# Fused attention and SwiGLU kernel: a third exp buffer, a lagged and re-timed prologue, and the second batch's attention placed earlier

## The chip, the cores and the metric

The kernel runs on one core of one Trainium2 chip. The metric is the device time of one execution in microseconds (us). Engines are named as the profile names them: PE is the matmul engine (PEld its weight loads), DVE is VectorE, ACT is ScalarE, POOL is GpSimd, SP is SyncE. In these traces PE, DVE, ACT and POOL each work through their own instructions in the order in which they were issued (in the hole shown below, a copy on DVE whose input was ready at 87.04 us began at 90.28 us, behind two scalings and a product).

## The reference

Attention over 8 batches, 12 heads, 448 positions and head size 64, with one extra term in the denominator, feeds a feed-forward network (FFN) on 3584 rows of 768:

```python
scores = scale * np.matmul(q, k.transpose(0, 1, 3, 2))
m = np.max(scores, axis=-1, keepdims=True)
e = np.exp(scores - m)
attn = e / (np.sum(e, axis=-1, keepdims=True) + np.exp(-m) + 1e-09)
o = np.matmul(attn, v)                                     # (8, 12, 448, 64)
x = o.transpose(0, 2, 1, 3).reshape(B * S, H * D)          # (3584, 768)
rms = np.sqrt(np.mean(x * x, axis=-1, keepdims=True) + 1e-06)
xn = x / rms * rms_g
g = xn @ w_gate                                            # 768 x 1536
silu = g * (1.0 / (1.0 + np.exp(-g)))
out = silu * (xn @ w_val) @ w_out                          # 1536 x 768
```

All inputs and the output are fp32. The kernel works in bf16 on PE.

## The kernel before

The program has a prologue and a main part. In the prologue the attention of batch 0 is computed alone, with dummy ("warm") matmuls at its start. The main part is the FFN, written as a list of steps: a gate or value step (`TA`, six matmuls of 448 columns, and a tanh on ScalarE for the gate) and an output step (`TB`, twelve matmuls of 384). A counter `now` adds up the steps' nominal lengths, and a timetable `ops` says at which value of `now` each piece of the other batches' attention is put between two FFN steps. I call the units of `now` FFN units, counted from the first FFN matmul. One is close to a microsecond of FFN work; the attention put between the steps comes on top (in the changed kernel the scaling set at 16.5 begins at 83.21 us, 43.8 us after the first FFN matmul).

The work of a head pair: transpose q and k on PE (`emit_T`) and copy the result out of PSUM (the memory that holds PE's results) on VectorE (`pair_t`); four chunks of scores on PE, each followed by one exp on ScalarE into `p_sb`; then the two heads' weighted sums on PE against v, which carries a column of ones for the denominator (`emit_AV`), and a reciprocal and a multiply on VectorE, which fill `x_sb`. After six pairs: sums of squares, a root, the scaling of x by row, transposes on PE, and then the FFN of that batch can start.

```python
    p_bufs = []
    v_bufs = []
    for i in range(2):
        p_i = consts.tile([128, C * 2 * S + PAD], BF16, name=f"p_sb{i}")
        nc.vector.memset(p_i[96:128, 0:2 * S + PAD], 1.0)
        nc.vector.memset(p_i[:, C * 2 * S:], 0.0)
        p_bufs.append(p_i)
        v_i = consts.tile([128, C, H, E1], BF16, name=f"v_sb{i}")
        # ... memsets of v_i ...
    # ... cut ...
        def exps():                                   # inside scores(g, c)
            p_v = p_bufs[g % 2][0:P, c * 2 * S:(c + 1) * 2 * S].rearrange("p (h q) -> p h q", h=2)
            nc.scalar.activation(out=p_v, in_=s_ps[0:P, :, 0:S], func=AF.Exp, scale=scale)
        return exps

    def emit_S(g, half):
        catch_up()
        pend = [scores(g, c) for c in (2 * half, 2 * half + 1)]
        pend[0]()
        put_off.append(pend[1])
        if not late[0]:
            catch_up()
    # ... cut ...
    def emit_scale(b, c):
        nc.vector.tensor_scalar(out=xn_tiles[b][:, c, :], in0=x_tiles[b][:, c, :],
                                scalar1=xnt_tiles[b, "r"][:, c:c + 1], scalar2=None,
                                op0=ALU.mult)
    # ... cut: the timetable; emit_T(6..13) and pairs 6..11 are batch 1 ...
    spans = {2: (24, 58), 3: (58, 90), 4: (90, 136), 5: (136, 172), 6: (172, 214), 7: (214, 251)}
    for j, t0 in enumerate((0.0, 1.2, 3.5, 5.8, 13.6, 15.9, 21.5, 25.0)):
        ops.append((t0, lambda j=j: emit_T(NP + j)))
    for j, t0 in enumerate((1.1, 3.4, 5.7, 8.0, 14.8, 17.1)):
        ops += [(t0 + 0.56 * i, op) for i, op in enumerate(micro_ops(NP + j))]
    ops.append((20.6, lambda: emit_stats(1, 1)))
    ops.append((20.7, lambda: emit_root(1)))
    ops.append((23.0, lambda: (emit_scale(1, 0), emit_scale(1, 1))))
    ops.append((24.1, lambda: (emit_scale(1, 2), emit_scale(1, 3))))
    for c in range(C):
        ops.append((25.2 + 0.01 * c if c < 2 else 26.3 + 0.01 * c, lambda c=c: emit_turn_x(1, c)))
    for i in range(2 * KD):
        ops.append((5.0 + 0.7 * i, lambda: scale_w(1)))
    # ... cut: casts on GpSimd, among them v, q and k of batch 2 at 22.5 to 22.7 ...
    now = 0.0
    for t, f in ffn:
        late[0] = t == TA
        while ops and ops[0][0] <= now:
            ops.pop(0)[1]()
        f()
        catch_up()
        # ... steps of later batches ...
        now += t
```

With `late` set, a step of two score chunks issues only its first exp; the second is held until after the next FFN step, so on ScalarE it stands behind that step's tanh.

The softmax here doesn't subtract the row's maximum and nothing guards it: scores larger than these inputs give would overflow.

## Time and profile before

| | before |
|---|---|
| median of the first 3 runs | 489.59 us (488.14 to 489.92) |
| span of the profiled run | 486.9 us, mean granted PE clock 0.986 |
| first FFN matmul | 41.91 us |
| PE idle in the hole at 81 to 95 us | 3.88 us, clock 0.88 |

The first part of the profile page gives busy time, share of the span and instruction count of each engine:

```profile
PE 462.1 (95%) x4041; PEld 248.1 (51%) x4041; DVE 247.3 (51%) x620; ACT 245.7 (50%) x357; POOL 101.4 (21%) x123
```

PE is the bound, with all others near half. So the question is where its last 5% goes. The windows view cuts the span into stretches of one's choosing. Its columns are: stretch, length, busy time of each engine (with instruction counts), granted PE clock (1.00 is full), DMA share, GB/s. For the prologue, the FFN of batch 0, the start of batch 1's FFN, and the last batches:

```profile
core 0: us, PE busy (x) PEld busy (x) DVE busy (x) ACT busy (x) POOL busy (x), PEclk, DMA share, GB/s
0.00:41.91 41.91, 32.40 (x401) 18.50 (x402) 27.75 (x79) 23.88 (x31) 25.75 (x41) 0.88 1.11 195
41.91:81.00 39.09, 38.83 (x439) 20.50 (x439) 27.20 (x67) 25.67 (x34) 7.55 (x10) 1.00 0.59 114
81.00:95.20 14.20, 10.32 (x92) 5.24 (x90) 11.28 (x22) 5.31 (x11) 12.19 (x15) 0.88 0.69 135
...
356.89:454.32 97.43, 96.26 (x709) 51.95 (x708) 45.73 (x110) 38.08 (x60) 2.68 (x4) 1.00 0.19 44
```

Length minus PE busy is PE's idle time: 9.51, 0.26, 3.88 and 1.17 us. The prologue and the hole stand out. The timeline shows the gap in each. Its columns are: start, duration, engine, line, operation, output and inputs with shapes, count, and in brackets the idle time before it with what ended that. First the prologue:

```profile
12.56 0.58 PE L174 MATMUL qkt_ps<-identity,k_bf 112*64 112x112 bf16 x8 [1.12 <-DMA k_bf<-in_k_dram]
...
13.68 0.92 ACT L206 ACTIVATE p_sb_117<-s_ps 112x896 bf16<-112x896 f32 x1 [2.38 <-PE s_ps L201]
...
27.78 3.34 ACT L206 ACTIVATE p_sb_117<-s_ps 112x896 bf16<-112x896 f32 x4
```

PE stands at the transposes of a head group whose k has not landed, and ScalarE has no scores for 2.38 us. The last exp of batch 0 ends at 27.78 + 3.34 = 31.12 us. Then the hole:

```profile
86.37 3.47 DVE L261 TENSOR_SCALAR xn<-x_sb,rinv 112x768 bf16<-112x768 bf16 x2
...
87.59 1.05 POOL L150 CAST q_bf<-q_f 112x1024 bf16<-112x1024 f32 x1
88.57 1.05 POOL L150 CAST k_bf<-k_f 112x1024 bf16<-112x1024 f32 x1
...
90.95 0.72 PE L270 MATMUL xnt_ps<-identity,xn 112*128 112x112 bf16 x6 [3.51 <-DVE pair_t_107 L177]
91.46 2.44 PE L302 MATMUL v_ps<-xnt_sb,wv_bf 128*128 128x448 bf16 x6
```

Two scalings of x take 3.47 us while GpSimd casts; the pair copy and the transposes queue behind them, PE waits 3.51 us, and its next six FFN matmuls take 2.44 us, about twice the 1.29 to 1.31 us of such a group elsewhere. The waits view of 300 to 490 us (engine, line, what it waited for, us in total, times, longest) has one longer wait and seven short ones of the kind of its second line here:

```profile
PE g_ps L302 <- DMA xnt_sb<-xn: 1.2, 1, 1.2
PE g_ps L302 <- DVE silu_5892 L308: 0.2, 1, 0.2
...
```

### The profile page before, as it was taken

What the parts mean: (1) busy time and instruction counts of PE and PEld (TensorE: products, weight loads), DVE (VectorE), ACT (ScalarE), POOL (GpSimd) and SP (SyncE); (2) the same over time, 40 slices, a digit from 0 to 9 for tenths busy, and PEclk for the clock granted to TensorE, in tenths of its full rate; (3) what the DMA queues carried; (4) which work ended last, traced back from release to release, by engine and by line L of the source; (5) the groups of instructions that cost most, each with busy time, mean ns of one, the idle gap of its engine ahead of it and who ended that gap; (6) DMA issues with size and microseconds to landing.
All of it is one profiled execution on the core that took longest, in us unless ns stands there. A gap on an engine that the chain in (4) does not pass through costs nothing.

```text
span 486.9 us, 9856 instructions
## 1 busy us (share of the span) xinstructions
PE 462.1 (95%) x4041; PEld 248.1 (51%) x4041; DVE 247.3 (51%) x620; ACT 245.7 (50%) x357; POOL 101.4 (21%) x123
## 2 busy tenths in 40 slices
PE   6988999799999999999999999999999999999995
PEld 2544555345455554544555554444555554455563
DVE  4586778645635166755633155745643156555200
ACT  4764755456556565545555655455556552122221
POOL 7454401801403031322003121313010001000000
PEclk9789999899999999999999999999999999999999
DMA  8999750999929997386039988189014320300133
GB/s 144 215 221 200 146 113 1 171 217 201 213 62 225 178 276 152 44 191 126 1 71 232 222 216 151 24 184 184 8 34 104 86 66 7 51 1 0 34 97 98
DMA packets 86905, 60.48 MB, mean 124 GB/s; under 512 B 50774, under 2 KB 81820, under 8 KB 86860
## 3 DMA queue, kind: packets, MB, share of 16 engines
q1 hardware_dynamic: 73820, 43.60, 42.2%
q0 software_dynamic: 13040, 16.26, 18.6%
q8 instruction: 31, 0.51, 0.5%
q14 instruction: 14, 0.11, 0.1%
HBM read 47.19 MB, written 11.01 MB: 120 GB/s over the span
## 4 chain that ended last, share of the span: by engine, by line
PE 81%; DVE 10%; ACT 3%; DMA 2%; issue 1%; POOL 1%; DVEq 0%; ACTq 0%; POOLq 0%
PE o_ps L327 23%; PE g_ps L302 19%; PE v_ps L302 18%; PE u_ps L231 9%; PE s_ps L201 8%; DVE xsq L254 3%; PE s_ps L302 3%; ACT t_sb L306 2%; DVE xn L261 1%; DMA k_bf<-in_k_dram 1%; DVE ht_sb L313 1%; DVE x_sb L235 1%; PE qkt_ps L174 1%; DMA xnt_sb<-xn 1%; ACT p_sb_117 L206 0%
## 5 line engine op out<-in xcount | busy, mean ns | idle before, releaser
L302 PE MATMUL v_ps<-xnt_sb,wv_bf 128*128 128x448 bf16 x576 | 126.0, 355 | 2.5 <-DVE ht_sb L313 2.4
L327 PE MATMUL o_ps<-wo_bf,ht_sb 128*128 128x384 bf16 x672 | 116.5, 326 | 0.4 <-DVE silu_2063 L308 0.4
L302 PE MATMUL g_ps<-xnt_sb,wg_bf 128*128 128x448 bf16 x504 | 109.3, 353 | 3.7 <-DMA xnt_sb<-xn 1.2
L206 ACT ACTIVATE p_sb_111<-s_ps 112x896 bf16<-112x896 f32 x96 | 84.0, 915 | 21.3 <-PE s_ps L201 21.2
L306 ACT ACTIVATE t_sb<-g_ps 128x448 f32<-128x448 f32 x84 | 45.6, 543 | 95.1 <-PE g_ps L302 94.8
L206 ACT ACTIVATE p_sb_117<-s_ps 112x896 bf16<-112x896 f32 x96 | 83.8, 915 | 16.8 <-PE s_ps L201 16.6
L327 PEld LDWEIGHTS <-ht_sb 128*128 128x128 bf16 x672 | 62.8, 98 | 46.8 <-issue 8.3
L302 PEld LDWEIGHTS <-wg_bf 128*128 128x128 bf16 x576 | 52.2, 97 | 58.4 <-issue 15.6
L302 PEld LDWEIGHTS <-wv_bf 128*128 128x128 bf16 x576 | 52.8, 98 | 54.8 <-issue 12.1
L330 ACT ACTIVATE out_sb<-o_ps 128x384 f32<-128x384 f32 x56 | 27.5, 490 | 66.4 <-PE o_ps L327 61.5
L234 DVE RECIPROCAL recip<-u_ps 112x4 f32<-112x4 f32 x96 | 17.0, 178 | 84.3 <-PE u_ps L231 84.3
L285 POOL TENSOR_TENSOR rinv<-ms,neghalf 112x2 f32<-112x2 f32 x16 | 10.9, 706 | 160.1 <-DVE ms L281 160.1
L235 DVE TENSOR_TENSOR x_sb<-u_ps,recip 112x256 bf16<-112x256 f32 x96 | 40.8, 424 | 3.3
L150 POOL CAST q_bf<-q_f 112x1024 bf16<-112x1024 f32 x17 | 17.7, 1041 | 100.0 <-DMA q_f<-in_q_dram 86.6
L201 PE MATMUL s_ps<-qk_t 64*128 64x448 bf16 x272 | 37.5, 354 | 0.0
L254 DVE CUSTOM_DVE_ANT_0 xsq<-x_sb 112x512 bf16<-112x512 bf16 (+1 forms) x60 | 36.7, 612 | 1.6
L231 PEld LDWEIGHTS <-p_sb_117 112*128 112x128 bf16 (+1 forms) x768 | 30.1, 99 | 11.7 <-issue 3.9
L231 PEld LDWEIGHTS <-p_sb_111 112*128 112x128 bf16 (+1 forms) x768 | 30.0, 99 | 9.8 <-issue 3.8
L150 POOL CAST k_bf<-k_f 112x1024 bf16<-112x1024 f32 x17 | 17.9, 1054 | 13.2 <-DMA k_f<-in_k_dram 13.2
L261 DVE TENSOR_SCALAR xn<-x_sb,rinv 112x768 bf16<-112x768 bf16 x32 | 19.8, 649 | 0.1
L201 PEld LDWEIGHTS <-qk_t 64*128 64x128 bf16 x272 | 7.8, 94 | 21.2 <-issue 20.4
L231 PE MATMUL u_ps<-v_sb_114,p_sb_117 112*128 112x65 bf16 (+1 forms) x384 | 16.9, 197 | 1.6 <-DVE x_sb L235 1.3
(265 smaller groups left out, 347.7 us busy)
## 6 DMA issues: line engine op xcount, KB each, us to landing
q_f<-in_q_dram SPq DMA_DIRECT2D x15, 448.0 KB, 4.8
k_f<-in_k_dram SPq DMA_DIRECT2D x15, 448.0 KB, 6.1
v_f<-in_v_dram SPq DMA_DIRECT2D x15, 448.0 KB, 7.0
v_f<-in_v_dram POOLq DMA_DIRECT2D x9, 448.0 KB, 7.8
out_dram<-out_sb SPq DMA_DIRECT2D x8, 336.0 KB, 3.4
wg_bf<-in_moe_w_gate_dram POOLq DMA_DIRECT2D x6, 384.0 KB, 11.5
wv_bf<-in_moe_w_val_dram POOLq DMA_DIRECT2D x6, 384.0 KB, 13.7
wo_bf<-in_moe_w_out_dram POOLq DMA_DIRECT2D x3, 768.0 KB, 18.1
```

The lines of the kernel that those rows point to most:

```text
L150: eng.tensor_copy(out=dst, in_=staged[n, i].rearrange("p h c d -> p c h d"))
L201: nc.tensor.matmul(s_ps[:, hh, 0:S], lhsT=k_t[r, k0:k0 + 128], rhs=qs[r], start=True, stop=True)
L206: nc.scalar.activation(out=p_v, in_=s_ps[0:P, :, 0:S], func=AF.Exp, scale=scale)
L231: nc.tensor.matmul(u_ps[:, qc, :], lhsT=p_sb[0:K, q0:q0 + 128], rhs=v_sb[0:K, c, h, :], start=(c == 0), stop=(c == C - 1))
L234: nc.vector.reciprocal(out=recip, in_=u_ps[0:P, :, D:E1])
L235: nc.vector.tensor_tensor(out=x_tiles[b][:, :, h * D:(h + 1) * D], in0=u_ps[0:P, :, 0:D], in1=recip.to_broadcast([P, C, D]), op=ALU.mult)
L254: nc.vector.tensor_tensor_reduce(out=xsq[:, 0:cols.stop - cols.start], in0=x_c, in1=x_c, scale=1.0, scalar=0.0, op0=ALU.mult, op1=ALU.add, ...
L261: nc.vector.tensor_scalar(out=xn_tiles[b][:, c, :], in0=x_tiles[b][:, c, :], scalar1=xnt_tiles[b, "r"][:, c:c + 1], scalar2=None, op0=ALU. ...
L302: nc.tensor.matmul(ps[:, 0:S], lhsT=w[:, dk, m * 128:(m + 1) * 128], rhs=xnt_tiles[b][:, :, dk, :], start=(dk == 0), stop=(dk == KD - 1))
L306: nc.scalar.activation(out=t, in_=ps[:, 0:S], func=AF.Tanh, scale=0.5)
L327: nc.tensor.matmul(o_ps[:, 0:HN], lhsT=ht_tiles[b2][:, fk, c * 128:(c + 1) * 128], rhs=wo_bf[:, fk, n * HN:(n + 1) * HN], start=(fk == 0), ...
L330: nc.scalar.activation(out=o_sb[:, n * HN:(n + 1) * HN], in_=o_ps[:, 0:HN], func=AF.Copy, scale=0.5)
```

## The change

Its intent: get batch 0 to its FFN sooner, by giving q and k of the next head groups the first place among the loads, letting the weighted sums run two pairs behind the scores (which needs a third exp buffer), and filling PE with dummy matmuls where it would idle; close the hole, by finishing batch 1 earlier, so that its scaling comes before GpSimd's casts; and let gate results go to the score banks as soon as the last scores are done. x is scaled in place, which saves a buffer. Cut to its core:

```diff
+    NPB = 3
-    for i in range(2):
+    for i in range(NPB):
         p_i = consts.tile([128, C * 2 * S + PAD], BF16, name=f"p_sb{i}")
         nc.vector.memset(p_i[96:128, 0:2 * S + PAD], 1.0)
 # ... v buffers: still two; weights loaded three 128-row blocks at a time instead of two ...
-    def scale_w(n):
+    def scale_w(n, eng):            # ScalarE or VectorE
 # ...
-            p_v = p_bufs[g % 2][0:P, ...]
+            p_v = p_bufs[g % NPB][0:P, ...]
 # ... sums of squares of batch 0 in three parts: heads 0-5, 6-9, 10-11 ...
-        nc.vector.tensor_scalar(out=xn_tiles[b][:, c, :], in0=x_tiles[b][:, c, :],
+        nc.vector.tensor_scalar(out=x_tiles[b][:, c, :], in0=x_tiles[b][:, c, :],
 # ...
-        if b == B - 1 and part == 0:
+        if scores_done[0] and part == 0:
             ps = ps_s.tile([128, 2, 512], FP32, name="s_ps")[:, 0, :]
 # ... the timetable ...
-    for j, t0 in enumerate((0.0, 1.2, 3.5, 5.8, 13.6, 15.9, 21.5, 25.0)):
+    for j, t0 in enumerate((2.3, 3.4, 5.6, 7.2, 8.8, 10.4, 18.6, 22.0)):
         ops.append((t0, lambda j=j: emit_T(NP + j)))
-    for j, t0 in enumerate((1.1, 3.4, 5.7, 8.0, 14.8, 17.1)):
-        ops += [(t0 + 0.56 * i, op) for i, op in enumerate(micro_ops(NP + j))]
-    ops.append((20.6, lambda: emit_stats(1, 1)))
-    ops.append((20.7, lambda: emit_root(1)))
-    ops.append((23.0, lambda: (emit_scale(1, 0), emit_scale(1, 1))))
-    ops.append((24.1, lambda: (emit_scale(1, 2), emit_scale(1, 3))))
+    for j, t0 in enumerate((4.0, 5.6, 7.2, 8.8, 10.4, 12.0)):
+        ops += [(t0 + 0.39 * i, op) for i, op in enumerate(micro_ops(NP + j))]
+    ops.append((14.9, lambda: (emit_stats(1, 1), emit_root(1))))
     for c in range(C):
-        ops.append((25.2 + 0.01 * c if c < 2 else 26.3 + 0.01 * c, lambda c=c: emit_turn_x(1, c)))
+        ops.append((16.5 + 0.6 * c, lambda c=c: emit_scale(1, c)))
+        ops.append((18.7 + 1.1 * c, lambda c=c: emit_turn_x(1, c)))
     for i in range(2 * KD):
-        ops.append((5.0 + 0.7 * i, lambda: scale_w(1)))
+        ops.append((9.0 + 0.45 * i, lambda: scale_w(1, V)))
-    # ... GpSimd: casts of batch 2 at 22.5 to 22.7 and 29.0
+    # ... GpSimd: casts of batch 2 at 19.5 and 19.6 and 26.0; load_w(4), the second
+    #     weight half, at 3.7 (before: in the prologue)
 # ... the prologue ...
+    between = {
+        (0, 0): [lambda: emit_T(1), lambda: [load_qkv(2, i, G) for i in range(2)]],
+        (0, 1): [gains, lambda: warm(1)], (0, 2): [lambda: warm(2)], (0, 3): [lambda: warm(2)],
+        (1, 0): [lambda: warm(2)], (1, 1): [lambda: warm(2)],
+        (1, 2): [lambda: emit_T(2), lambda: cast_qkv(0, 2, V)],
+        # ...
+        (2, 1): [lambda: emit_AV(0, 0)], (2, 2): [lambda: emit_AV(0, 1)],
+        # ... and so on, two pairs behind the scores ...
+    }
     for g in range(NP):
-        for op in micro_ops(g):
-            op()
+        for c in range(C):
+            scores(g, c)()
+            for f in between[g, c]:
+                f()
```

The transposes of batch 1's first pair (0.0 before, 2.3 after) move from just before the first FFN matmul to behind it.

## The prediction

> **What bounds the kernel now.** The matmul engine (PE). By the windows view it is busy 32.4 of the first 41.9 us (before the first FFN matmul), 38.8 of the next 39.1, 10.3 of 14.2 between 81.0 and 95.2 us, and 380.6 of the last 391.8 (some 5 us of that idle is the tail). Apart from dummy warm-up matmuls, PE work is the same after the change. So three things can move the time: the start of the first FFN matmul (41.9 us), the hole at 81 to 95 us, and small PE waits elsewhere.
>
> **Prologue.** ScalarE runs 24 exps, 0.81 us each back to back, from 7.1 us. In the timeline they end at 31.1 us, though 24 x 0.81 = 19.5: some 4 us are lost, 2.4 where PE stood at the third pair's transposes until q and k of the second head group landed (12.5 us), the rest mostly because PE then ran at half clock (mean 0.66 from 10 to 20 us; 16 weighted-sum matmuls took 1.0 us against 0.6 later). The Trainium skill (TensorE: Matmul & The Clock Gate, "What's actually happening") says idle PE is re-throttled; the trace agrees. The change loads v later, transposes later, adds warm-up matmuls and lags the weighted sums, so exps lose that gap. The price: a third exp buffer puts one more 0.8 us VectorE memset ahead of the first transposed copy (+1 us); VectorE is nearly full from 20 to 31 us (0.55 us per head's scaling, copies 0.54, casts 0.60, squares 0.46 to 0.72), and the last pair's copy queues among squares, so the last exps slip 1 to 2 us. The chain after the last weighted sum (sums, root, scaling 4 x 0.73 us, transposes) stays about 8 us. First FFN matmul: 39.0 us (37.5 to 40.5), gain 2.9.
>
> **Hole.** VectorE's scaling of x took 1.7 us a piece there against 0.73 in the prologue, while GpSimd ran casts; PE waited 3.5 us and its clock fell (six matmuls 2.24 us instead of 1.14). Whole loss about 5.3 us. The Trainium skill (GPSIMD Engine Reference, "1. Specifications") says GpSimd shares its SBUF interfaces with VectorE; 1.7 against 0.73 us fits. The change finishes batch 1 some 6 FFN units earlier and puts scaling ahead of the casts: gain 5 us.
>
> **Given back.** Batch 1's attention is pressed from 19 into 10 FFN units. There PE needs about 22 us and ScalarE 21 (24 exps, 4 tanh of 0.45): I expect 2 us (0.5 to 4) of new PE waits for exps. The second weight half lands near 60 us, needed at 59 to 66: no wait, little slack.
>
> **Elsewhere.** Gate results move to the score banks one batch earlier: seven waits of 0.2 us go; one of 1.2 us for transposed x should go: about -2 us. Scaling in place adds no wait.
>
> **Sum.** 489.6 - 2.9 - 5 + 2 - 2 = 481.7 us; range 477.5 to 486. Faster by over 2% 0.27, within 2% 0.71, slower 0.02.
>
> **What would show it.** Right: no 2.4 us gap between exps; first FFN matmul near 39 us; waits for exps of 1 to 3 us in the first 25 us of the FFN; no PE wait over 1 us up to 110 us; no waits on silu in the last two batches. Wrong: first FFN matmul after 41 us, or PE waiting for weight scaling.
>
> **What would make it wrong.** First-half weights landing after 31 us; the dense stretch costing 4 us or more; VectorE less full in the prologue than I think (then 478); another hole at batch 1's transposes.

## The result, and the profile after

Ratios here and below are the mean time of one kernel's runs over the mean of the other's runs of the same rounds, so not quite the ratio of the medians.

| | before | after |
|---|---|---|
| median (runs) | 489.75 us (488.14 to 489.92, 4) | 485.76 us (485.36 to 486.50, 4) |
| ratio, 95% interval | | 0.9927 [0.9903, 0.9952] |
| span of the profiled run | 486.9 us, clock 0.986 | 483.3 us, clock 0.994 |
| first FFN matmul | 41.91 us | 39.41 us |

The change gains about 3.6 us by the ratio (0.0073 x 489), where 7.9 were forecast. Busy times by engine after:

```profile
PE 460.6 (95%) x4053; PEld 247.9 (51%) x4056; DVE 242.0 (50%) x625; ACT 250.6 (52%) x363; POOL 98.4 (20%) x119
```

That page line hardly moves, so the averages are no help. The windows view of the same stages does show it (columns as before):

```profile
0.00:39.41 39.41, 31.43 (x397) 16.90 (x401) 25.94 (x81) 27.30 (x35) 18.60 (x32) 1.00 1.00 178
39.41:79.06 39.65, 34.20 (x415) 18.58 (x415) 23.69 (x61) 25.59 (x34) 11.38 (x15) 0.96 0.74 142
79.06:95.20 16.14, 14.63 (x126) 7.50 (x123) 12.25 (x29) 7.54 (x14) 11.12 (x13) 1.00 0.48 113
...
356.97:451.21 94.24, 94.24 (x706) 51.98 (x705) 45.31 (x108) 38.12 (x60) 2.68 (x4) 1.00 0.18 45
```

PE's idle time is now 5.45 us in the FFN of batch 0 (0.26 before), 1.51 in the former hole (3.88 before), and none in the last batches (1.17 before). The waits view of 39 to 110 us names the new idle time:

```profile
PE s_ps L205 <- ACT p_sb_108 L210: 2.2, 3, 1.1
PE s_ps L205 <- ACT p_sb_111 L210: 1.4, 3, 0.6
PE u_ps L235 <- DVE x_sb L239: 1.3, 1, 1.3
PE s_ps L205 <- DVE pair_t_102 L181: 1.1, 1, 1.1
```

With one more of 0.21 us, seven waits for exps sum to 3.8 us. The timeline at their worst place shows the queue on ScalarE:

```profile
46.27 0.92 ACT L210 ACTIVATE p_sb_108<-s_ps 112x896 bf16<-112x896 f32 x1 [2.03 <-PE s_ps L205]
46.35 1.31 PE L310 MATMUL g_ps<-xnt_sb,wg_bf 128*128 128x448 bf16 x6
...
47.69 0.54 ACT L314 ACTIVATE t_sb<-g_ps 128x448 f32<-128x448 f32 x1 [0.51 <-PE g_ps L310]
48.13 2.52 ACT L210 ACTIVATE p_sb_108<-s_ps 112x896 bf16<-112x896 f32 x3
...
49.10 0.37 PE L205 MATMUL s_ps<-pair_t_102 64*128 64x448 bf16 x2 [1.14 <-ACT p_sb_108 L210]
...
50.71 0.55 PE L205 MATMUL s_ps<-pair_t_104 64*128 64x448 bf16 x2 [0.44 <-ACT p_sb_108 L210]
51.19 2.42 PE L310 MATMUL v_ps<-xnt_sb,wv_bf 128*128 128x448 bf16 x6
```

ScalarE waits 2.03 us for the first scores of the pair, does one exp, idles another 0.51 us for the gate, and only then meets three exps in a row, for which PE has to wait: there are two score banks, and both are full. It was idle 2.5 us just before it became the bottleneck. The six matmuls at 51.19 took 2.42 us, so PE's clock had also been halved.

The hole is nearly gone. One wait is left there, for the copy of a transposed pair (the last line of this cut of the timeline; the lines before it show scalings of x and a cast):

```profile
83.21 0.42 DVE L266 TENSOR_SCALAR x_sb<-x_sb,rinv 112x768 bf16<-112x768 bf16 x1 [0.20 <-POOL rinv L293]
...
83.80 1.03 POOL L154 CAST v_sb_117<-v_f 112x1024 bf16<-112x1024 f32 x1
84.07 2.08 DVE L266 TENSOR_SCALAR x_sb<-x_sb,rinv 112x768 bf16<-112x768 bf16 x2
...
87.85 0.55 PE L205 MATMUL s_ps<-pair_t_102 64*128 64x448 bf16 x4 [1.15 <-DVE pair_t_102 L181]
```

So the scaling of x did not get ahead of GpSimd's casts, as the change intended. Only the first scaling came before them; the next two took 2.08 us under the cast of v and one of q from 84.78 us, and the last took 0.66 us, from 86.61. The four together took 3.16 us, against 1.48 + 3.47 = 4.95 us before.

In the waits view of 300 to 490 us PE's only entry is this one; the seven silu waits and the DMA wait are gone:

```profile
PE v_ps L310 <- DVE ht_sb L321: 0.4, 1, 0.4
```

The start of the prologue and the first FFN matmul, in the timeline:

```profile
7.55 0.36 PE L205 MATMUL s_ps<-pair_t_102 64*128 64x448 bf16 x2 [1.02 <-DVE pair_t_102 L181]
...
7.95 3.34 ACT L210 ACTIVATE p_sb_108<-s_ps 112x896 bf16<-112x896 f32 x4 [4.30 <-PE s_ps L205]
...
29.32 1.82 ACT L210 ACTIVATE p_sb_114<-s_ps 112x896 bf16<-112x896 f32 x2 [0.41 <-PE s_ps L205]
...
39.41 1.29 PE L310 MATMUL g_ps<-xnt_sb,wg_bf 128*128 128x448 bf16 x6 [0.69 <-DVE xnt_sb L280]
```

The exps start 0.81 us later than before (7.95 against 7.14), have no gap of 2.38 us any more, and still end at the same time: 29.32 + 1.82 = 31.14 against 31.12 us. ScalarE's waits for scores after the first exp sum to 2.45 us (0.74, 0.23, 1.07, 0.41), against 3.74 before (2.38, 0.56, 0.57, 0.23); the later start and small gaps take up the rest. So the 2.5 us by which the FFN starts earlier come after the exps. By the timeline, the last weighted sum ends 1.15 us after the last exp (2.48 before), three weight scalings no longer stand on VectorE ahead of the last squares, the four scalings of x take 2.19 instead of 2.97 us, and 0.5 us of transposes has moved behind the start.

### The profile page after: what moved, and what is told of

Same layout as the page of the kernel before. It is cut to its first block, busy times and chain, and to the rows that moved or that the text cites. A ratio compares the mean times of both kernels' runs of the same rounds, so it can differ in the third digit from the quotient of the medians.

```text
span 483.3 us, 9859 instructions
## 1 busy us (share of the span) xinstructions
PE 460.6 (95%) x4053; PEld 247.9 (51%) x4056; DVE 242.0 (50%) x625; ACT 250.6 (52%) x363; POOL 98.4 (20%) x119
## 4 chain that ended last, share of the span: by engine, by line
PE 80%; issue 8%; DVE 6%; POOL 3%; ACT 2%; POOLq 0%; DVEq 0%
PE o_ps L335 23%; PE v_ps L310 19%; PE g_ps L310 15%; PE u_ps L235 8%; PE s_ps L205 8%; PE s_ps L310 5%; DVE xsq L261 2%; PE warm_ps L354 2%; DVE x_sb L239 1%; DVE ht_sb L321 1%; POOL v_sb_120 L154 1%; ACT t_sb L314 1%; PE qkt_ps L178 1%; ACT wg_bf L119 1%; DVE pair_t_102 L181 0%
## 5 line engine op out<-in xcount | busy, mean ns | idle before, releaser
L310 PE MATMUL g_ps<-xnt_sb,wg_bf 128*128 128x448 bf16 x444 | 96.3, 353 | 1.1 <-DVE xnt_sb L280 0.7
L314 ACT ACTIVATE t_sb<-g_ps 128x448 f32<-128x448 f32 x74 | 40.2, 543 | 73.3 <-PE g_ps L310 73.1
L261 DVE CUSTOM_DVE_ANT_0 xsq<-x_sb 112x256 bf16<-112x256 bf16 (+3 forms) x64 | 36.0, 563 | 1.7
L314 ACT ACTIVATE t_sb<-s_ps 128x448 f32<-128x448 f32 x22 | 11.9, 543 | 38.5 <-PE s_ps L310 33.3
L310 PE MATMUL s_ps<-xnt_sb,wg_bf 128*128 128x448 bf16 x132 | 28.6, 352 | 0.0
```

The costliest lines, as they stand in the source:

```text
L261: nc.vector.tensor_tensor_reduce(out=xsq[:, 0:n], in0=x_c, in1=x_c, scale=1.0, scalar=0.0, op0=ALU.mult, op1=ALU.add, accum_out=acc)
L310: nc.tensor.matmul(ps[:, 0:S], lhsT=w[:, dk, m * 128:(m + 1) * 128], rhs=xnt_tiles[b][:, :, dk, :], start=(dk == 0), stop=(dk == KD - 1))
L314: nc.scalar.activation(out=t, in_=ps[:, 0:S], func=AF.Tanh, scale=0.5)
```

## The experiments

Three rivals for the missing gain: (A) batch 1's attention is pressed into so few FFN units that exps come in bursts; (B) the bursts come from the held exp, which stands behind a tanh; (C) VectorE is overloaded by the scaling of the second weight half, which falls in the same stretch. Later a fourth: (D) the prologue does not give its gain in every run. All twelve kernels ran in 5 rounds against the kernel before, in three batches of four. The median of before was 489.27, 488.54 and 488.57 us in the three. No result was wrong but one.

### Batch 1 spread over 14 units

```diff
-    for j, t0 in enumerate((4.0, 5.6, 7.2, 8.8, 10.4, 12.0)):
-        ops += [(t0 + 0.39 * i, op) for i, op in enumerate(micro_ops(NP + j))]
-    ops.append((14.9, lambda: (emit_stats(1, 1), emit_root(1))))
+    for j, t0 in enumerate((4.0, 6.1, 8.2, 10.3, 12.4, 14.5)):
+        ops += [(t0 + 0.52 * i, op) for i, op in enumerate(micro_ops(NP + j))]
+    ops.append((18.2, lambda: (emit_stats(1, 1), emit_root(1))))
 # scaling 16.5 -> 19.6, transposes 18.7 -> 21.4, casts of batch 2 19.5 -> 22.5,
 # DMA transposes 23.0 -> 26.0 and the rest of batch 2's loads likewise
```

> The changed kernel with batch 1's attention spread from 10 to about 14 FFN units, its statistics, scaling and transposes 3 units later and the GpSimd casts behind them. The changed kernel stands at 485.8 us, with 5.4 us of matmul-engine idle and a throttled clock (mean 0.96) between 39.4 and 79 us. Theory A (packing asks for exps faster than ScalarE can give them): that idle falls to 2 us or less, the clock there is 1.00, time 481.5 us (480 to 483.5). Theory B (the second exp of each pair of chunks is held behind the next tanh on ScalarE): the waits for exps largely stay, 484 us or more. Theory C (VectorE's queue is full of weight scaling): about 484 us, with the waits on x_sb and pair copies left.

Measured: 492.28 us (491.82 to 494.66), ratio 1.0073 [1.0046, 1.0101]: slower than before. That is a fault of the experiment. Moving the casts along with the rest left batch 2 without its transposed q and k, and PE waited 9.62 us for them at 112.7 us. It neither supports nor refutes A; the next kernels mend it.

### No held exp in the stretch

```diff
-        late[0] = t == TA
+        late[0] = t == TA and now > 15.5
```

> The changed kernel as it is, but up to FFN unit 15.5 each exp is issued right behind its scores, never held back behind the next FFN step's tanh. Theory A (capacity): little changes, 485.3 us (484.5 to 486.5), waits for exps still 3 us. Theory B (order on ScalarE): the first waits (1.14 and 0.44 us near 48 to 51 us) and the throttling after them go, idle under 2.5 us, time 482.5 us.

Measured: 485.34 us (483.08 to 488.15), ratio 0.9924 [0.9890, 0.9958], where after has 0.9927. The six times spread over 5.1 us and show no gain, but the trace shows one. In the stretch after the first FFN matmul the waits for exps sum to 1.7 us instead of 3.8, the longest 0.4 us; PE idles 4.40 us instead of 5.45, and the clock there stays full. In exchange the wait for `x_sb` grows from 1.3 to 2.1 us. So holding the exp isn't the whole cause, as B had it (idle time under 2.5 us, 482.5 us), but it is a part of it; the table after the next two runs shows how large a part.

### Second weight half not scaled (a wrong result)

```diff
-        ops.append((9.0 + 0.45 * i, lambda: scale_w(1, V)))
+        pass
```

> The changed kernel without the scaling of the second weight half by the gain on VectorE (a wrong result on purpose: 12 operations of 0.33 to 0.41 us fewer in batch 1's attention). Theories A and B: only the 1.3 us wait on x_sb near 78 us goes, 484.5 us (483.5 to 485.5), the waits for exps stay. Theory C (VectorE full): 482.5 us or less.

Measured: 485.38 us (483.74 to 488.20), ratio 0.9920 [0.9890, 0.9950]; relative error 0.71, as meant. In its trace the waits for exps are unchanged at 3.8 us, and the wait of 1.3 us for `x_sb` is gone from this stretch. C falls as the cause of the bursts.

### Spread and no held exp

> Both edits: batch 1 spread, exps not held in it. Theory A: the same as the spread one alone within 0.7 us, 481.5 us. Theory B: at least 1.5 us faster than the spread one alone.

Both edits above together. Measured: 491.32 us (489.74 to 493.76), ratio 1.0041 [1.0013, 1.0070], again with the late casts' wait, in the timeline:

```profile
108.14 0.93 PE L205 MATMUL s_ps<-qk_t 64*128 64x448 bf16 x4 [9.76 <-DMA qk_t<-k_bf]
```

But the stretch that was in dispute can be read by itself. The windows view of this kernel:

```profile
39.40:60.00 20.60, 20.16 (x228) 10.09 (x228) 12.11 (x28) 14.31 (x20) 10.92 (x14) 1.00 0.69 121
60.00:79.00 19.00, 17.85 (x235) 10.28 (x232) 15.40 (x44) 12.97 (x20) 0.88 (x2) 1.00 0.82 166
```

PE idles 0.44 + 1.15 = 1.59 us there, at full clock, against 5.46 us with clock 0.92 in its first half for the changed kernel in the same two windows. ScalarE does as much work, only more evenly. But this kernel has both edits. To tell them apart, take the 39.65 us from the first FFN matmul on in each profile:

| kernel | PE idle | waits for exps |
|---|---|---|
| changed kernel | 5.45 us | 3.8 us |
| exps not held | 4.40 us | 1.7 us |
| spread, exps held: the first spread, and the next run | 2.13 and 2.40 us | 2.1 and 2.1 us |
| spread, exps not held | 1.59 us | 0.3 us |

(The two in the third row had a clock of 0.96 and 0.93 there.) Each edit alone takes away about half of the waits for exps, and both together nearly all. So A stands, with B as a part of it: the bursts come from the dense timetable together with the held exp, and most of the idle time goes with the density.

### Spread, with the casts in time

```diff
 # as the spread above, but the casts and loads of batch 2 earlier:
-                 (10.5, lambda: loads(2 * NG + 1)), (19.5, lambda: cast_qkv(2 * NG, 2, G)),
-                 (19.6, lambda: casts(2 * NG + 1)), (19.7, lambda: loads(2 * NG + 2)),
-                 (23.0, lambda: turn_qk(2 * NG + 1)), (26.0, lambda: casts(2 * NG + 2)),
-                 (29.0, lambda: turn_qk(2 * NG + 2))):
+                 (10.5, lambda: loads(2 * NG + 1)), (15.0, lambda: cast_qkv(2 * NG, 2, G)),
+                 (15.1, lambda: casts(2 * NG + 1)), (15.2, lambda: loads(2 * NG + 2)),
+                 (19.0, lambda: turn_qk(2 * NG + 1)), (24.0, lambda: casts(2 * NG + 2)),
+                 (27.0, lambda: turn_qk(2 * NG + 2))):
```

> The spread of the first run again, but the GpSimd casts and transposed loads of batch 2's second head group are now moved ahead (FFN unit 15 to 19) instead of behind (22.6 to 26), which in the first run cost one 9.6 us wait for qk_t. Exps still held behind the next tanh. Theory A (packing against ScalarE's rate): no wait over 2 us after 60 us, waits for exps between FFN start and 80 us about 2 us instead of 3.6, time 482.5 us (481 to 484.5) where the changed kernel has 485.7. Theory A falls if it stays above 485 us with the long wait gone.

Measured: 483.77 us (481.54 to 485.32), ratio 0.9898 [0.9868, 0.9928]. The waits for exps fall from 3.8 to 2.1 us (1.14, 0.35, 0.64). The direction is A's; by the ratios it is about 1.4 us better than after (0.0029 x 489), and the intervals of the two overlap.

### The same without the held exp

```diff
-        late[0] = t == TA
+        late[0] = t == TA and now > 18.5
```

> The same with exps issued right behind their scores in batch 1. Its profile should show under 1 us of waits for exps between FFN start and 80 us and a full clock there (in the fourth run's profile this edit left 0.35 us). Theory A: 481.5 us, 0.5 to 1.5 below the one that holds exps. Theory B (holding is what matters): 2 us or more below it.

Measured: 486.57 us (481.08 to 492.59). Three of the six runs count as slow, being over 1.5% above the fastest, so the ratio 0.9876 [0.9834, 0.9917] rests on three runs; I call it inconclusive. Its trace is of use all the same. Waits for exps are down to 0.35 us, but PE waits 2.65 us for `x_sb`, because the early casts on GpSimd now lie under VectorE's squares. The timeline of VectorE and GpSimd there:

```profile
71.12 1.04 POOL L154 CAST v_sb<-v_f 112x1024 bf16<-112x1024 f32 x1 [8.55 <-DMA v_f<-in_v_dram]
71.21 1.17 DVE L121 TENSOR_SCALAR wv_bf<-wv_bf,gain 128x768 bf16<-128x768 bf16 x1
...
72.96 0.69 DVE L261 CUSTOM_DVE_ANT_0 xsq<-x_sb 112x512 bf16<-112x512 bf16 x1
73.17 1.38 POOL L154 CAST q_bf<-q_f 112x1024 bf16<-112x1024 f32 x1 [1.01 <-DMA q_f<-in_q_dram]
...
73.69 1.40 DVE L261 CUSTOM_DVE_ANT_0 xsq<-x_sb 112x512 bf16<-112x512 bf16 x1
...
75.96 1.04 POOL L154 CAST k_bf<-k_f 112x1024 bf16<-112x1024 f32 x1 [1.41 <-DMA k_f<-in_k_dram]
76.10 1.44 DVE L261 CUSTOM_DVE_ANT_0 xsq<-x_sb 112x512 bf16<-112x512 bf16 x1
```

Add start and duration. The first cast ends at 72.16, the weight scaling under it at 72.38; the second cast at 74.55, the square at 75.09; the third at 77.00, the square at 77.54. Both squares end 0.54 us after their cast, whenever they began, and one that no cast had reached first took 0.69. That looks like a VectorE instruction that does next to nothing until the cast is over. The Trainium skill (SBUF — State Buffer, "Who interferes with whom") describes just this: VectorE and GpSimd have one pair of ports to SBUF (the on-chip memory in which the tiles lie) in common, held by one instruction at a time, and the other is blocked outright rather than slowed. This trace agrees. The page says also that a VectorE instruction with at most one SBUF input, outside its two-port modes, isn't touched; in the hole of the kernel before, a silu product and a pair copy, which read PSUM, each took their usual 0.61 us wholly or mostly under a cast of v.

### The two halves of the change apart

One kernel has the new prologue with the old timetable and gate banks; the other the old prologue (two buffers, a separate `xn`) with the new timetable and gate banks.

```diff
 # new prologue, old timetable (against the changed kernel)
-        if scores_done[0] and part == 0:
+        if b == B - 1 and part == 0:
-    for j, t0 in enumerate((4.0, 5.6, 7.2, 8.8, 10.4, 12.0)):
-        ops += [(t0 + 0.39 * i, op) for i, op in enumerate(micro_ops(NP + j))]
+    for j, t0 in enumerate((1.1, 3.4, 5.7, 8.0, 14.8, 17.1)):
+        ops += [(t0 + 0.56 * i, op) for i, op in enumerate(micro_ops(NP + j))]
 # ... spans, emit_T, stats, scaling, transposes, casts as before;
 # the scaling of the second weight half keeps its new times ...
```

> The prologue half of the change alone: three exp buffers, weighted sums two pairs behind, loads, weights split, scaling in place, but the old timetable of the FFN phase and the old gate banks. If the prologue is worth its 2.0 to 2.5 us and the packed timetable loses about as much as it gains, this is at 486 to 487.5 us: the old hole near 85 us (waits of 3 us or more on the pair copy) is back and there is no wait for exps over 0.5 us before it. If the packed timetable is a net gain of 3 us or more, this is at 489 us or above.

Measured: 489.92 us (485.66 to 492.03), ratio 1.0016 [0.9978, 1.0055]: no gain at all, and outside the expected 486 to 487.5 us. By the other branch of that expectation (489 us or above) the new timetable is a net gain of 3 us or more; by the ratios the whole change is 0.0089 x 489 = 4.4 us better than this kernel. The profile fell on the fastest of the six runs, the only one with a clock of 1.000; the others had 0.981 to 0.989. Even in it the hole is back; the timeline shows the same wait as before:

```profile
89.94 0.46 PE L275 MATMUL xnt_ps<-identity,x_sb 112*128 112x112 bf16 x6 [3.50 <-DVE pair_t L181]
```

> The timetable half alone: the old prologue, two exp buffers and separate scaled x, with the packed FFN timetable and gate results in the score banks. Expected 487.5 us (486.5 to 489): the hole shrinks by 3 to 4 us and 3 us of small waits go in the later batches, but 4 to 6 us of waits for exps and a throttled clock come in the 35 us after the FFN starts.

Measured: 486.73 us (485.47 to 490.08), ratio 0.9975 [0.9937, 1.0012]. The windows view of its FFN of batch 0:

```profile
40.65:80.00 39.35, 34.03 (x415) 18.60 (x416) 22.87 (x58) 23.83 (x31) 8.41 (x11) 0.96 0.59 117
```

PE idles 5.32 us here with clock 0.96, as in the changed kernel (5.45 us, 0.96), and the seven exp waits have nearly the same lengths (3.9 us in all). So the loss in this stretch belongs to the new timetable alone; the prologue, the third buffer and the scaling in place have no part in it. The two ratios don't multiply to that of the whole change (0.9991 against 0.9927); each interval is some 0.004 wide on either side, and I leave it there.

### The changed kernel once more, as a control

> The changed kernel itself again, on this chip and in these rounds, because the runs so far vary by 3 to 6 us with the granted clock. Expected median 486 us, lowest 485, highest up to 489; in the profile either a full clock from 6 us on and a first FFN matmul at 39.4 us, or a half clock for some microseconds after the wait for the first pair copy (6.2 to 7.5 us) and a first FFN matmul at 40.8 to 43.3 us.

Measured: 485.26 us (484.24 to 488.97), ratio 0.9941 [0.9897, 0.9985]. So four runs at first had made the kernel look steadier than it is. The ten runs of the changed kernel, time and mean granted clock of each:

```
first batch   485.56 0.994   486.50 0.989   485.97 0.991   485.36 0.996
control       488.97 0.981   484.25 0.996   484.80 0.996   485.73 0.992   484.24 0.996   487.16 0.990
```

The time follows the clock. The four at 0.996 average 484.7 us, all ten 485.9: 1.2 us of the average are lost to a clock that falls in some runs. The slowest was the profiled one, and its trace shows where:

```profile
7.53 0.56 PE L205 MATMUL s_ps<-pair_t 64*128 64x448 bf16 x2 [2.04 <-DVE pair_t L181]
...
10.62 1.03 PE L354 MATMUL warm_ps<-blank 128*128 128x512 bf16 x2
10.72 0.92 ACT L210 ACTIVATE p_sb<-s_ps 112x896 bf16<-112x896 f32 x1 [0.31 <-PE s_ps L205]
...
12.18 0.92 ACT L210 ACTIVATE p_sb<-s_ps 112x896 bf16<-112x896 f32 x1 [0.54 <-PE s_ps L205]
...
43.30 1.29 PE L310 MATMUL g_ps<-xnt_sb,wg_bf 128*128 128x448 bf16 x6 [0.69 <-DVE xnt_sb L280]
```

The wait for the first pair's copy is 2.04 us here and 1.02 in the first profile, although the scores begin at the same time, 7.53 and 7.55 us. The copy's time is set by VectorE, which has the memsets of the third exp buffer (0.82 us) and of v ahead of it; PE came to it earlier. Why, the record of the granted clock in the two traces shows. (It has no entry for the first microseconds of a run, and the views count these as full, but the dummy matmuls then run at half speed: ten take 4.45 us in the first profile.) The first full clock came at 3.87 us here and at 6.39 in the first profile, so that the eight transposes of q took 0.39 us here and 0.58 there. With the longer wait the clock was then halved, by the record from 7.29 to 14.11 us: a score chunk took 0.56 instead of 0.36 us, and the two fill matmuls that the change put between chunks 1.03 instead of 0.61. Together that is more than one exp, so exps start 1.46 us apart (10.72, 12.18) instead of 0.81, and the first FFN matmul comes at 43.30 us, 3.9 us later than in the first profile. A second stretch at half clock, from 31.18 to 38.01 us, has a part in that: the exps are 2.7 us late before it (26.10 against 23.40 us) and 3.7 us at their end (34.86 against 31.14).

Nine profiles have exactly the changed kernel's prologue: the two of that kernel itself, that of the new prologue with the old timetable, and those of the six kernels that came before it in this section. In them the start of the FFN ranges from 39.3 to 43.3 us; this wait was 1.02 to 1.18 us in the three that started by 39.4 and 1.40 to 2.06 in the six that started at 40.8 or later. The first full clock came at 6.03 to 6.39 us in the three and at 3.86 to 5.48 us in the six. This supports D: how much of the prologue's gain is had depends on the run, and in these profiles on when the first full clock came. The kernel before is no steadier: in the rounds of the control its eleven runs range from 486.68 to 493.43 us.

### The wait bridged by more dummy matmuls

```diff
     emit_T(0)
+    warm(5)
```

> The changed kernel with five more dummy matmuls behind the first pair's transposes, where the matmul engine otherwise waits 1.0 to 2.1 us for VectorE (whose queue holds one more exp-buffer memset than before the change). Theory D (this wait lets the clock gate close, and the half clock then stretches the distance of exps from 0.81 to 1.2 to 1.5 us): full clock from 8 us on in the profile, first FFN matmul near 39.5 us, highest timed run within 2.5 us of the lowest, mean 1 to 2 us below the control's. If the gate is not closed by this wait, mean and range are the control's.

Measured: 484.96 us (483.68 to 485.20), ratio 0.9916 [0.9879, 0.9953]. The runs lie within 1.5 us where the control's spread over 4.7, all at a clock of 0.994 to 0.996, and the mean is 484.6 us, which is what the four best-clocked runs of the changed kernel had (484.7). That supports the halved clock after this wait as the source of the spread. The profile by itself is no test: in it the first full clock came at 7.03 us, later than in all nine, so that the wait would have been short without the bridge. The next run has the better one.

### The memsets moved behind the first pair's copy

```diff
+    fill_p(0)                 # only the first exp buffer is filled at the start
     # ...
     emit_T(0)
+    fill_p(1)
+    warm(3)
     # ...
-        (0, 0): [lambda: emit_T(1), lambda: [load_qkv(2, i, G) for i in range(2)]],
+        (0, 0): [lambda: emit_T(1), lambda: fill_p(2), lambda: [fill_v(i) for i in range(2)],
+                 lambda: [load_qkv(2, i, G) for i in range(2)]],
```

> The changed kernel with the memsets of the second and third exp buffer and of both v buffers moved behind the first pair copy, and three dummy matmuls there. Theory D and the queue on VectorE: first scores at about 6.9 us instead of 7.5, first exp at 7.3 instead of 7.95, first FFN matmul at 38.8 us (38.2 to 39.3), full clock from there on, mean 1.5 to 2.5 us below the control's.

Measured: 484.09 us (483.26 to 484.70), ratio 0.9903 [0.9867, 0.9940]; range 1.4 us. Against the control of the same batch the mean is 1.9 us lower; how much of that is the clock is not shown, as the mean clocks of the six runs hardly differ (0.993 and 0.992). In its profile the first full clock came at 4.31 us, as early as in the six unlucky ones, and it was kept through the place of the wait: that early clock does no harm once the wait is gone. The first exp begins at 6.68 instead of 7.95 us. The FFN nevertheless starts at 39.5 us (38.2 to 39.3 was expected), no earlier than the lucky runs of the changed kernel; the clock fell later, from 28.20 to 35.03 us.

### Late memsets and the spread together

The kernel above, with the spread, the casts at 16.5 and 16.6 (between the two places tried), their DMA transposes at 20, the transposes of batch 2's first pair at 17.0 instead of 18.6, and no held exp in the first 7 units:

```diff
-        late[0] = t == TA
+        late[0] = t == TA and now > 7.0
```

> All that helped, put together: late memsets, batch 1 spread over 14 units, casts of the next head group between its last weighted sum and its scaling (not during its squares, which took 1.40 instead of 0.68 us under casts), exps of its first pair not held, the next batch's first transposes 1.6 units earlier. Expected 480 us (478.5 to 482), ratio to the kernel before 0.982; the waits for exps between FFN start and 80 us under 1.2 us, no throttling there, no 1.15 us wait for the pair copy near 86 us.

Measured: 479.80 us (478.64 to 481.66, five runs), ratio 0.9825 [0.9778, 0.9872]. All its runs are faster than all of the changed kernel's and of before's; the interval excludes 1 but not a gain below 2%. Against the late memsets alone the mean is 4.1 us lower, in the same batch. The windows view, and in the timeline the longest exp wait left:

```profile
39.09:79.00 39.91, 38.13 (x459) 20.56 (x460) 27.96 (x71) 26.70 (x37) 18.34 (x22) 1.00 0.83 158
```

```profile
69.53 0.36 PE L208 MATMUL s_ps<-pair_t 64*128 64x448 bf16 x2 [0.64 <-ACT p_sb L213]
```

PE idles 1.78 us of the stretch in which the changed kernel idles 5.45 us. ScalarE has no less to do (26.70 against 25.59 us). This version beats both kernels.

## Why the prediction was right or wrong

The time is inside the range, by 0.2 us, and the class (within 2%) was the likeliest named. The expected gain of 7.9 us was not had; it was 3.6. Of the sum, term by term, by the two profiles:

| term | forecast | profiles |
|---|---|---|
| start of the FFN | -2.9 | -2.5, of which 0.5 only moved (in a run whose clock held) |
| hole | -5 | -4.1 |
| given back in batch 1's attention | +2 (0.5 to 4) | +6.3 to +6.8 |
| elsewhere | -2 | -2.9 |

With the start counted as -2.0, the other terms (+6.8 for the third) and 0.5 us by which the last 32 us became shorter give -2.7 us, against -3.6 between the two profiled spans; 0.9 us I can't assign.

**Given back: the term that failed, in size.** The step that failed is "I expect 2 us (0.5 to 4) of new PE waits for exps". The mechanism (waits for exps after pressing 19 units into 10) was named; the amount was not. The waits for exps came to 3.8 us, nearly double; 1.3 us of waiting for `x_sb` and 1.1 to 1.6 us of half clock were not in the forecast at all. So the term was 4.3 to 4.8 us too small, as much as the whole shortfall of 4.3 us, and the prediction had listed "the dense stretch costing 4 us or more" among what would make it wrong. Measured: idle time rose from 0.26 to 5.45 us, and one group of six matmuls lost 1.1 us to the halved clock (2.42 against 1.31); taking the clock of 0.96 over all of the 39.65 us gives at most 1.6. The prediction had compared averages: "PE needs about 22 us and ScalarE 21". Two engines that are both nearly full and feed each other through two banks get by on that only when each one's work is evenly laid, and ScalarE idled 2.03 + 0.51 us before its first burst. The spread with the same work brought the idle time to 2.13 and 2.40 us, with the exps not held as well to 1.59 and 1.78, and the timetable alone on the old prologue brought it to 5.32: that the cause is the timetable's density, the runs show. They show too that the held exp has a part in it (without it 1.7 us of waits for exps instead of 3.8), which the prediction did not name, and that weight scaling has none in the bursts: without it only the wait for `x_sb` goes. The prediction also left out that new waits halve the clock, though it had read just that in the old hole.

**Prologue: size nearly right in a good run, the place wrong, and not had in every run.** "Exps lose that gap": the gap of 2.38 us went, and the exps ended at 31.14 us all the same, against 31.12. The later start (0.81 us, forecast as 1) and the slip at the last copies (waits of 1.07 and 0.41 us, forecast as 1 to 2) ate it; these two were right one by one, but not seen to cancel the whole. "The chain after the last weighted sum ... stays about 8 us" was wrong in our favour: it went from 8.3 us (33.60 to 41.91) to 7.1 (32.29 to 39.41). That the start is a lottery was not foreseen. The third buffer's memset was priced at its own length; that PE waits behind it and may lose its clock was not. Bridging the wait brought the runs together; that is shown. How early PE comes to the wait is set by the first full clock, between 3.86 and 6.39 us in the nine profiles; what sets that moment in a given run, no run here shows.

**Hole: right in size, not in how.** Idle time and clock cost 3.88 us and at most 0.12 x 14.2 = 1.7 us before, and 1.51 us after. The wait of 3.5 us is gone, but the scaling did not come ahead of the casts: it began at 83.21 us (84.44 before), the casts at 83.80 (84.34 before), and two of the four scalings took 2.08 us. Set one by one, the four took 3.16 us instead of 4.95, and the copy that PE waits for began at 87.18 instead of 90.28 us. Whether the finer setting did it or the little that batch 1 came earlier, no run separates. "No PE wait over 1 us up to 110 us" was wrong: 1.15 us for a pair copy, 1.31 for `x_sb` and 1.14 for exps are left, and 1.02 twice in the prologue. And the base of 0.73 us for a scaling, taken from the old prologue, was itself a contended one: two v casts ran there (2.97 us for four scalings). Alone, two of them take 0.74 us (at 86.22 us in the spread with the casts in time). The Trainium skill (GPSIMD Engine Reference, "1. Specifications") says the two engines share their SBUF interfaces, and the traces agree: 1.75 us each in the hole, nearly five times the free duration, not two and a half.

**Elsewhere: right.** The seven silu waits and the DMA wait of 1.2 us are gone; with the new prologue and the old timetable and gate banks they are there (nine, and 1.2 us), with the new timetable and banks alone they are not. Summed from 95 us to the tail, PE's idle time fell from 6.0 to 3.1 us. "Scaling in place adds no wait" held, and PE never waited for weight scaling by more than 0.2 us at the start of the FFN.

**The clock.** The Trainium skill (TensorE: Matmul & The Clock Gate, "What's actually happening") says that PE is slowed after an idle window of about 3.4 us, and that the window is free-running, so that the moment varies from run to run. The window is in these traces: each stretch at one clock that the records show before the end of a run lasts a multiple of 3.41 us (in the control the clock changes at 3.87, 7.29, 14.11, 31.18 and 38.01 us), and the moments differ from run to run. But a window need not be idle throughout: in the prologue the clock was halved after waits of 1.40 to 2.06 us and kept after waits of up to 1.18 us. Nor does the length of one wait decide it. In the hole of the new prologue with the old timetable PE waited 3.50 us and kept the full clock; the wait fell on two windows, with PE idle for 1.51 us of the first (84.53 to 87.95 us) and 1.99 us of the second. In the kernel before, a wait of 3.51 us put 3.1 us of idle time into one window (87.14 to 90.56 us), and the clock was halved. As 1.99 us did no harm here and 1.40 us did there, idle time alone gives no limit either (the ends of matmuls are modelled in the profile, so these sums are rough); what else counts stays open.

## What to carry to other kernels

Averages over a stretch say nothing of bursts: before pressing work together, write down for each in-order queue what stands behind what, and ask where the engine that will be the bottleneck idles just before. A start-up wait of one or two microseconds behind a memset can cost several more through the clock (here up to 3.9), and not in every run, so bridge it or shorten the queue in front of it, and compare kernels over many runs. Put GpSimd's casts between VectorE's SBUF-to-SBUF work, not under it, and when one item of a timetable moves, check who needs its result: the first spread lost more than it won in that way.

## What the Trainium skill lacked or had wrong

- TensorE: Matmul & The Clock Gate: the page speaks of idle time over about 3.4 us. The window is there, but it need not be idle throughout. Here a single wait of 1.40 us or more in the prologue was followed by the half clock in six of six profiles, one of 1.02 to 1.18 us in none of three; and two waits of 1.14 and 0.44 us with 1.2 us of work between them were followed by 2.42 us for a group of six matmuls that otherwise takes 1.31, while a wait of 3.50 us that fell on two windows left the clock full. Its section "A second HAM failure mode: psum-queue depth-cycling" says that frequent short idle times can do it, but with no size.
- The same page puts the cost of the slow clock at the start at under 1% of a typical span. That holds here, but it isn't negligible for a tuned kernel: the start of the FFN moved between 39.3 and 43.3 us with it, and the runs of one kernel lay between 484.2 and 489.0 us, which is more than the whole change gains.
- SBUF — State Buffer gives the port rule and two slow-downs (6.8 and 1.5 times), but not for which instructions. Here 112 x 1024 casts on GpSimd (1.03 to 1.38 us) took squares of 112 x 512 from 0.69 to 1.40 and 1.44 us, one weight scaling from 0.41 to 1.17 us, and scalings of 112 x 768 from 0.37 to 1.75 us.
